# Attention with a gated feed-forward block on one core: pairs of token tiles by another seven-product scheme with two gathering PSUM banks, and a whole first gate

## The chip, the cores and the metric

The kernel runs on one NeuronCore of a Trainium2 chip. The core has five engines that run their own queues in order: TensorE (PE; its weight loads are shown apart as PEld), VectorE (DVE), ScalarE (ACT), GpSimd (POOL) and SyncE (SP, which here issues DMAs). The metric is the device time of one execution in microseconds; lower is better.

## The reference

Attention with a window of 96 positions and 8 global positions, then a feed-forward block with a ReLU gate on its output:

```python
B, H, S, D = 4, 8, 768, 64                 # q, k, v; n_global 8, n_local 96
keep = is_global | is_local
scores = scale * q @ k.T + bias            # bias: -slope of the head * distance
a = softmax(np.where(keep, scores, -1e9))
x = (a @ v) as [3072, 512]                 # tokens x (heads * 64)
gate = np.maximum(x @ w_gate, 0.0)         # w_gate, w_val: [512, 1536]
val = x @ w_val
out = (gate * val) @ w_out                 # w_out: [1536, 512], result fp32
```

## The kernel before

The 3072 tokens are cut into eight halves c = 0 to 7 (half a sequence each, 384 tokens, three tiles of 128). Per half there are two stages.

*Attention of a half* (`attention_pieces`): for each of four pairs of heads, scores on TensorE into `x_ps` banks (L397), Exp on ScalarE (L406), masks on VectorE (L359), the product with the values and its row sums on TensorE (L427), the reciprocal of the sums as Ln (L436) and Exp (L441) on ScalarE, and two multiplications on VectorE that normalise the result into the transposed activations `xT` (L446).

*Feed-forward of a half* (`ffn_pieces`): twelve chunks fc of 128 hidden columns. `gate(fc)` is four matmuls over `xT` into an `ff_ps` bank and a ReLU on ScalarE (L525). `val(fc)` is four matmuls and a multiplication on VectorE (L531) that writes `ht`, the hidden activations in bf16. Matmuls of both are at L518. Then comes the output product with w_out (`wo_sb`):

- the third token tile by 12 plain matmuls of 512 columns (`outp`, L538), copied out by ScalarE (L543); half 0 does all three tiles so
- the first two token tiles together by Strassen's scheme: the two tiles and the two halves of w_out's rows and columns make a 2x2 problem, done with 7 products of 6 matmuls of 256 columns (`block`, L583) in place of 8. VectorE makes sums of `ht` beforehand (`cb`, `ad`, `de`; L567, L571, L576), and, once, five sums of w_out (`bs`, L809). Products p4, p3, p1 are copied to the output tile `osb` by ScalarE (L599, L603, L607); p2 and p5 are added and subtracted there by VectorE (L611 to L617); p6 and p7 go on accumulating in the banks of p3 and p1 and are added last (L624, L629). They run in the order p4, p3, p1, p2, p5, p6, p7.

Halves 2 to 7 begin with `begin`: three quarters of gate 0 and of val 0 by turns, then the last quarter of each.

PSUM holds three `ff` and five `x` banks of 128x512 fp32. Buffers are handed out by turns, so an allocation waits until the one three (five) before it is read.

The order of all work is written by hand. `ffn_pieces(c)` gives a list of (weight, function); `weave` calls them in order and, when the summed weight passes a place, calls the attention pieces of the next half (`spread` gives their places, up to 0.8 of half c) and the loads and key transposes of the half after it (`early_pieces`, 0.25 to 0.75). Sums of `ht` stand behind certain `val` pieces (`behind`) or between output pieces (`f2.insert`). Each engine's queue is in this order: an instruction that waits holds all behind it. Output tiles are stored by SP's DMA queue; in half 7 one of four stores is on ScalarE's.

Of the kernel before, what the change touches and what calls it, by code (L numbers as in the profile page):

```python
# [8 lines left out]
FP32 = mybir.dt.float32  # L9
BF16 = mybir.dt.bfloat16  # L10
AF = mybir.ActivationFunctionType
ALU = mybir.AluOpType
# [3 lines left out]
def kernel(  # L16
# [12 lines left out]
    nc = tc.nc  # L29
# [14 lines left out]
    NHALF = 2 * B  # L44
# [27 lines left out]
    late = {}  # L72

    PSUM = bass.MemoryType.PSUM
    psum = {}
# [20 lines left out]
    wo_sb = const.tile([128, N_FC, DM], BF16)  # L96
# [409 lines left out]

    begin_of = {}

    def ffn_pieces(c):
        ht = ht_pool.tile([128, N_FC, QH], BF16, name="ht")  # L510
        st = {}
# [38 lines left out]
            if c == 2:  # L550
                product(wg, "g", 1, 0, N_DC - 1)


        N2, D2 = N_FC // 2, DM // 2
        tiles_ = [slice(n * 128, (n + 1) * 128) for n in range(2)]

        def sums_of(name, *shape):
            if name not in st:
                st[name] = late["sums"].tile([128, *shape], BF16, name=name)
            return st[name]  # L560

        cb = lambda: sums_of("cb", N2, 2, 128)
        ad = lambda: sums_of("ad", N2, 128)
        de = lambda: sums_of("de", N_FC, 128)

        def sum_cb(i0, i1):
            nc.vector.tensor_tensor(cb()[:, i0:i1].rearrange("f i n t -> f i (n t)"), ht[:, i0:i1, 0:256],  # L567
                                    ht[:, N2 + i0 : N2 + i1, 0:256], op=ALU.add)

        def sum_ad(i0, i1):  # L570
            nc.vector.tensor_tensor(ad()[:, i0:i1], ht[:, i0:i1, tiles_[0]],  # L571
                                    ht[:, N2 + i0 : N2 + i1, tiles_[1]], op=ALU.add)

        def sum_de(i0, i1):
            x, y = (1, 0) if i0 < N2 else (0, 1)
            nc.vector.tensor_tensor(de()[:, i0:i1], ht[:, i0:i1, tiles_[x]], ht[:, i0:i1, tiles_[y]],  # L576
                                    op=ALU.subtract)

        def block(key, pool, left, right, start, stop):
            if start:  # L580
                st[key] = psum[pool].tile([128, 512], FP32, name=f"{pool}_ps")
            for i in range(N2):
                nc.tensor.matmul(st[key][:, 0:D2], lhsT=left(i), rhs=right(i),  # L583
                                 start=start and i == 0, stop=stop and i == N2 - 1,
                                 skip_group_check=not start)
            return st[key][:, 0:D2]

        c0, c1 = slice(0, D2), slice(D2, DM)
        bs = lambda name: lambda i: late["bs"][name][:, i]
        V2 = nc.vector.tensor_tensor  # L590

        def store(n, cols, eng=nc.sync):
            eng.dma_start(out=out_v[c, n][:, cols], in_=st["r", n][:, cols])

        def p4():
            for n in range(2):
                st["r", n] = late["osb"].tile([128, DM], FP32, name="osb")
            ps = block("d", "ff", lambda i: ht[:, N2 + i, tiles_[1]], bs("b21-b11"), True, True)
            nc.scalar.copy(st["r", 0][:, c0], ps)  # L599

        def p3():
            ps = block("c", "ff", lambda i: ht[:, i, tiles_[0]], bs("b12-b22"), True, True)
            nc.scalar.copy(st["r", 0][:, c1], ps)  # L603

        def p1():
            ps = block("a", "ff", lambda i: ad()[:, i], bs("b11+b22"), True, True)
            nc.scalar.copy(st["r", 1][:, c1], ps)  # L607

        def p2():
            ps = block("b", "x", lambda i: cb()[:, i, 1], lambda i: wo_sb[:, i, c0], True, True)  # L610
            V2(st["r", 1][:, c0], ps, st["r", 0][:, c0], op=ALU.add)  # L611
            V2(st["r", 1][:, c1], st["r", 1][:, c1], ps, op=ALU.subtract)

        def p5():
            ps = block("e", "x", lambda i: cb()[:, i, 0], lambda i: wo_sb[:, N2 + i, c1], True, True)
            V2(st["r", 0][:, c1], ps, st["r", 0][:, c1], op=ALU.add)
            V2(st["r", 0][:, c0], st["r", 0][:, c0], ps, op=ALU.subtract)  # L617
            if c == NHALF - 1:
                store(1, c0)
                store(0, c1)  # L620

        def p6():
            ps = block("c", "ff", lambda i: de()[:, i], bs("b11+b12"), False, True)
            V2(st["r", 1][:, c1], ps, st["r", 1][:, c1], op=ALU.add)  # L624
            store(1, slice(0, DM) if c < NHALF - 1 else c1, nc.sync if c < NHALF - 1 else nc.scalar)

        def p7():
            ps = block("a", "ff", lambda i: de()[:, N2 + i], bs("b21+b22"), False, True)
            V2(st["r", 0][:, c0], ps, st["r", 0][:, c0], op=ALU.add)  # L629
            store(0, slice(0, DM) if c < NHALF - 1 else c0)  # L630

        behind = {2: [lambda: sum_de(0, 3)], 5: [lambda: sum_de(3, 6)], 8: [lambda: sum_cb(0, 3)],
                  9: [lambda: sum_ad(0, 3)], 10: [lambda: sum_de(6, 9)]}

        def val_and_sums(fc):
            val(fc)
# [8 lines left out]
        f2 = [(0.65, lambda n=n, part=part: outp(n, part))  # L645
              for n in (range(NN) if c < 1 else (NN - 1,)) for part in range(4)]
# [135 lines left out]
    for f in ("m1 g0 m3 v0 m2 g1 K3 K2 m0 g3 K1 S30 S31 g2 K0 S20 v3 S11 v1 S21 A3 N3 v2 S00 S01 "  # L782
# [10 lines left out]
        else:  # L793
# [8 lines left out]
    late["bs"] = {name: pool.tile([128, N_FC // 2, DM // 2], BF16, name=f"bs{i}")  # L802
                  for i, name in enumerate(("b21-b11", "b12-b22", "b11+b22", "b11+b12", "b21+b22"))}

    def wo_sum(name, part):
        i = slice(part * N_FC // 4, (part + 1) * N_FC // 4)
        x, y = (wo_sb[:, (int(b[1]) - 1) * N_FC // 2 :][:, i, (int(b[2]) - 1) * DM // 2 : int(b[2]) * DM // 2]
                for b in (name[:3], name[4:]))
        nc.vector.tensor_tensor(late["bs"][name][:, i], x, y, op=ALU.add if "+" in name else ALU.subtract)  # L809
# [9 lines left out]
    for f in (*casts[:7], lambda: nc.gpsimd.tensor_copy(held, wo_sb[0:1, N_FC - 1, 0:1]),  # L819
# [8 lines left out]
    weave(f1_0[G[2]] + f1_1[G[2]] + f2_0 + f2_1 + [(0.0, pieces.pop()[1])],  # L828
          [(0.33, order_k[2]), (0.38, order_k[3])],
          pieces, spread(early_pieces(3), 0.58, 0.88),  # L830
          spread([(0.0, lambda name=name, part=part: wo_sum(name, part)) for name in late["bs"] for part in range(2)],
                 0.1, 0.74))

    for c in range(2, NHALF):
        placed = []
        if c + 1 < NHALF:
            placed.append(spread(attention_pieces(c + 1), *((0.07, 0.82) if c == 2 else (0.0, 0.8))))
        if c + 2 < NHALF:
            load_qk(c + 2, 0, H)
            load_v_half(c + 2)  # L840
            placed.append(spread(early_pieces(c + 2), 0.25, 0.75))
        f1, f2 = ffn_pieces(c)
        weave(f1 + f2, *placed)

# [34 lines left out]
```

## Time and profile before

| | |
|---|---|
| median of 3 runs | 241.96 us (241.34 to 242.21) |
| the profiled execution | 241.74 us, of it 239.9 us from first to last instruction |
| granted TensorE clock | 0.998 of full speed |
| first matmul of the products of halves 1 to 7 | 71.8, 100.0, 126.9, 154.6, 181.6, 209.1, 231.9 us |
| first gate of halves 3 to 7 | 104.6, 131.5, 159.2, 186.2, 213.7 us |
| gate and val matmuls (L518) | 768, 53% of the chain that ended last |
| plain output product (L538) | 9% of that chain |
| Strassen products (L583) | 294 matmuls, 11% of that chain |
| VectorE: ht (L531), mean of one | 96, 554 ns |
| VectorE: output additions (L611 to L629) | 42, 409 to 425 ns |
| ScalarE: relu (L525), mean of one | 96, 492 ns |
| ScalarE: copies of products (L599, L603, L607) | 21, 370 to 374 ns |

In a line of the timeline the columns are the start in us from the span's beginning, the length in us, the engine, the line of the kernel, the operation, output<-input, and the shape; several like instructions that follow each other are one line with their count. In a line of stretches they are the stretch, its length, then for each engine its busy time and instructions (PE, PEld, DVE, ACT, POOL), the granted clock, the share of the DMA engines and GB/s. In the chain of waits they are start, length, engine, output, line and count. Matmuls are pipelined: one starts before the one ahead of it has ended.

### The profile page before, as it was taken

To read this page: it belongs to the slowest core of one execution; us is meant where nothing else is said; L and a number is where in the kernel's file an instruction comes from. 1 tells how busy PE (TensorE), PEld (TensorE's weight loads), DVE (VectorE), ACT (ScalarE), POOL (GpSimd) and SP (SyncE) were. 2 spreads that over 40 slices of the span, in tenths; PEclk is the share of its full clock that TensorE was granted. 3 is DMA by queue.
4 is the path that set the end of the run, shared out by engine and by line. 5 is a ranking of instruction groups with operands and counts; after the bars stand their busy time and mean duration, and the time that the engine had idled before them with its cause. 6 is when DMAs were issued, how large, how long until landed. Compare 5 with 4: busy or idle time off the path is not lost.

```text
span 239.9 us, 5355 instructions
## 1 busy us (share of the span) xinstructions
PE 233.5 (97%) x1937; PEld 146.6 (61%) x1945; DVE 173.3 (72%) x456; ACT 153.4 (64%) x347; POOL 85.9 (36%) x202
## 2 busy tenths in 40 slices
PE   7899999999999999999999999999999999999994
PEld 3655555665458566666668566676658566676663
DVE  7775955869677788777787687866887677764643
ACT  5897883337775777748774777638774677733330
POOL 6767893208414860903274060902350000000000
PEclk9999999999999999999999999999999999999999
DMA  6999999993976997098519939398431200030003
GB/s 200 181 198 177 257 234 219 185 162 61 270 178 134 301 150 131 8 185 257 108 25 122 285 93 133 19 166 262 67 68 44 90 0 0 3 129 3 4 27 104
DMA packets 69603, 31.42 MB, mean 131 GB/s; under 512 B 47160, under 2 KB 66616, under 8 KB 69576
## 3 DMA queue, kind: packets, MB, share of 16 engines
q0 software_dynamic: 31744, 8.71, 35.3%
q1 hardware_dynamic: 36616, 21.45, 35.1%
q10 hardware_dynamic: 1216, 0.92, 1.2%
q8 instruction: 15, 0.25, 0.4%
q14 instruction: 12, 0.10, 0.1%
HBM read 28.41 MB, written 6.29 MB: 145 GB/s over the span
## 4 chain that ended last, share of the span: by engine, by line
PE 91%; ACT 3%; DVE 2%; issue 1%; ACTq 0%
PE ff_ps L518 53%; PE ff_ps L538 9%; PE ff_ps L583 8%; PE x_ps L427 6%; PE x_ps L397 4%; PE x_ps L583 3%; PE t_ps L459 2%; PE s_ps L341 2%; PE t_ps L272 1%; PE t_ps L682 1%; ACT lnd L436 1%; PE t_ps L310 1%; DVE xT L446 1%; PE s_ps L321 1%; ACT rcp L441 0%
## 5 line engine op out<-in xcount | busy, mean ns | idle before, releaser
L518 PE MATMUL ff_ps<-xT,wg 128*128 128x384 bf16 x384 | 80.7, 326 | 0.5 <-ACT grelu L525 0.4
L518 PE MATMUL ff_ps<-xT,wv 128*128 128x384 bf16 x384 | 80.2, 326 | 0.0
L531 DVE TENSOR_TENSOR ht<-ff_ps,grelu 128x384 bf16<-128x384 f32 x96 | 53.1, 554 | 28.5 <-PE ff_ps L518 13.8
L525 ACT ACTIVATE grelu<-ff_ps 128x384 bf16<-128x384 f32 x96 | 47.1, 492 | 39.4 <-PE ff_ps L518 20.9
L518 PEld LDWEIGHTS <-wg 128*128 128x128 bf16 x384 | 35.9, 98 | 23.9 <-issue 0.9
L518 PEld LDWEIGHTS <-wv 128*128 128x128 bf16 x384 | 36.1, 97 | 23.4 <-issue 1.2
L406 ACT ACTIVATE es<-x_ps 128x360 bf16<-128x360 f32 (+2 forms) x96 | 36.8, 444 | 16.9 <-PE x_ps L397 16.8
L359 DVE TENSOR_TENSOR es<-es,m_all 128x432 bf16<-128x432 bf16 (+4 forms) x108 | 31.2, 334 | 8.2 <-ACT es L406 7.8
L446 DVE TENSOR_TENSOR xT<-x_ps,rcp 64x384 bf16<-64x384 f32 x48 | 26.6, 554 | 9.4 <-ACT rcp L441 8.8
L436 ACT ACTIVATE lnd<-x_ps 64x384 f32<-64x384 f32 x48 | 23.3, 485 | 12.5 <-PE x_ps L427 11.8
L538 PE MATMUL ff_ps<-wo_sb,ht 128*128 128x512 bf16 x112 | 29.6, 379 | 0.4
L363 POOL CAST kqc<-ks 128x384 bf16<-128x384 f32 x24 | 11.6, 532 | 32.3 <-DMA ks<-in_k_dram 32.3
L137 POOL DMA_DIRECT2D vbuf<-in_v_dram x25 | 21.6, 880 | 2.6 <-DMA wv<-in_moe_w_val_dram 2.1
L427 PE MATMUL x_ps<-es,vbuf 128*128 128x216 bf16 (+4 forms) x216 | 21.8, 225 | 0.0
L427 PEld LDWEIGHTS <-vbuf 128*128 128x128 bf16 x216 | 15.8, 97 | 7.7
L538 PEld LDWEIGHTS <-ht 128*128 128x128 bf16 x120 | 10.8, 97 | 9.8 <-issue 0.2
L263 POOL COPY kT<-kqT 128x240 bf16<-128x240 bf16 x16 | 6.9, 430 | 23.0 <-DMA kqT<-kqc 20.5
L363 POOL CAST kqc<-qs 128x384 bf16<-128x384 f32 x24 | 11.6, 522 | 8.1 <-DMA qs<-in_q_dram 8.1
L259 POOL COPY kT<-kqT 128x360 bf16<-128x360 bf16 x10 | 6.0, 604 | 19.9 <-DMA kqT<-kqc 19.9
L441 ACT ACTIVATE rcp<-lnd 128x384 f32<-128x384 f32 x24 | 12.6, 524 | 0.7
L347 ACT ACTIVATE ef<-s_ps 128x720 bf16<-128x720 f32 (+2 forms) x16 | 10.9, 710 | 2.1 <-PE s_ps L341 1.8
L397 PE MATMUL x_ps<-kqT,kT 64*128 64x216 bf16 (+4 forms) x216 | 11.8, 224 | 0.2
(115 smaller groups left out, 252.8 us busy)
## 6 DMA issues: line engine op xcount, KB each, us to landing
out_dram<-osb SPq DMA_DIRECT2D x22, 256.0 KB, 2.7
ks<-in_k_dram SPq DMA_DIRECT2D x6, 768.0 KB, 5.5
qs<-in_q_dram SPq DMA_DIRECT2D x6, 768.0 KB, 12.1
vbuf<-in_v_dram POOLq DMA_DIRECT2D x21, 120.0 KB, 7.9
wg<-in_moe_w_gate_dram POOLq DMA_DIRECT2D x3, 512.0 KB, 7.9
wv<-in_moe_w_val_dram POOLq DMA_DIRECT2D x3, 512.0 KB, 9.8
wo_sb<-in_moe_w_out_dram POOLq DMA_DIRECT2D x1, 1536.0 KB, 19.6
kq<-in_q_dram ACTq DMA_DIRECT2D x2, 192.0 KB, 4.7
```

The source lines that it names most:

```text
L137: nc.gpsimd.dma_start(out=v_dst(b, NG + r0, NG + r0 + n, j), in_=v[b, :, KT * j + r0 : KT * j + r0 + n, :].rearrange("h p d -> p h d"))
L359: nc.vector.tensor_mul(for_all, for_all, mk)
L363: nc.gpsimd.tensor_copy(kqc[:, :, i].rearrange("t n (h d) -> t h n d", d=D)[:, 2 * p : 2 * p + 2], of[s][:, 2 * p : 2 * p + 2, :].rearrang ...
L406: nc.scalar.activation(es[:, e, 0:c], banks[e][:, 0:c], AF.Exp, bias=0.0, scale=scale)
L427: nc.tensor.matmul(av3[:, :, a : a + w], lhsT=vb[:, j, z0 : z0 + 128], rhs=es[:, e, c : c + NN * w].rearrange("k (n p) -> k n p", n=NN), s ...
L436: nc.scalar.activation(ln[o0 : o0 + 64], av[d0 : d0 + 64, 0:QH], AF.Ln, bias=0.0, scale=1.0)
L446: nc.vector.tensor_tensor(xT_of[s][r, p, :], av_of[s, p, e][r, 0:QH], av_of[s, p, "r"][r], op=ALU.mult)
L518: nc.tensor.matmul(st[key][:, 0:QH], lhsT=w_of(w, dc, fc), rhs=xT_of[c][:, dc, :], start=(dc == 0), stop=(dc == N_DC - 1))
L525: nc.scalar.activation(gr, psg[:, 0:QH], AF.Relu, bias=0.0, scale=1.0)
L531: nc.vector.tensor_tensor(ht[:, fc, :], psv[:, 0:QH], st["gr", fc], op=ALU.mult)
L538: nc.tensor.matmul(ps2, lhsT=ht[:, fc, n * 128 : (n + 1) * 128], rhs=wo_sb[:, fc, :], start=(fc == 0), stop=(fc == N_FC - 1))
L583: nc.tensor.matmul(st[key][:, 0:D2], lhsT=left(i), rhs=right(i), start=start and i == 0, stop=stop and i == N2 - 1, skip_group_check=not s ...
```

## The change

The seven products follow another scheme (`winograd`): four sums s1 to s4 of `ht` and four sums t1 to t4 of w_out, each partly built on the one before, and four additions to the output. Three products (m1, m2 and m4) use a token tile as it is, three (m1, m2, m3) a part of w_out as it is. Products 6 and 7 accumulate onto product 1 in its bank, product 3 onto product 5 in its bank (`block` with `start` False); ScalarE copies out the states in between (m1, m5, m6, and m4), VectorE does the additions. Banks "a" and "b" are `ff` banks, "c" and "d" are `x` banks. The order is 1, 5, 6, 4, 2, 7, 3, and 1, 5, 6, 4, 7, 2, 3 in half 7. Sums stand at other places. Halves 3 to 7 begin with an ordinary gate 0 and val 0; half 2 keeps `begin`. The output pool has four buffers for three. A path for pairing third tiles is there, switched off by `PAIRED = ()`.

```diff
+    def winograd(pair, sums, order):
...
+        def add(j, i0=0, i1=N2):
+            lower, upper = slice(i0, i1), (N2 + i0, N2 + i1)
+            x, y, op = {1: lambda: (h(1, i0, i1), h(1, *upper), ALU.add),
+                        2: lambda: (s(1)[:, lower], h(0, i0, i1), ALU.subtract),
+                        3: lambda: (h(0, i0, i1), h(1, i0, i1), ALU.subtract),
+                        4: lambda: (h(0, *upper), s(2)[:, lower], ALU.subtract)}[j]()
+            V2(s(j)[:, lower], x, y, op=op)
...
+        def block(key, left, right, start=True):
+            if start:
+                pool = "ff" if key in "ab" else "x"
+                st[key] = psum[pool].tile([128, 512], FP32, name=f"{pool}_ps")
+            for i in range(N2):
+                nc.tensor.matmul(st[key][:, 0:D2], lhsT=left(i), rhs=right(i),
+                                 start=start and i == 0, stop=i == N2 - 1, skip_group_check=not start)
+            return st[key][:, 0:D2]
...
+        def m1():
+            nc.scalar.copy(r(0, 0), block("a", raw(0, 0), of_b(0, c0)))
+
+        def m2():
+            V2(r(0, 0), block("c", raw(0, 1), of_b(1, c0)), r(0, 0), op=ALU.add)
+            if last:
+                store(0, c0, nc.scalar)
+
+        def m3():
+            V2(r(0, 1), block("b", of_s(4), of_b(1, c1), False), r(0, 1), op=ALU.add)
+            store(0, c1 if last else slice(0, DM))
+
+        def m4():
+            nc.scalar.copy(r(1, 0), block("d", raw(1, 1), of_t(4)))
+
+        def m5():
+            nc.scalar.copy(r(1, 1), block("b", of_s(1), of_t(1)))
+
+        def m6():
+            nc.scalar.copy(r(0, 1), block("a", of_s(2), of_t(2), False))
+
+        def m7():
+            ps = block("a", of_s(3), of_t(3), False)
+            V2(r(1, 0), ps, r(1, 0), op=ALU.subtract)
+            V2(r(1, 1), ps, r(1, 1), op=ALU.add)
+            store(1)
+
+        return add, [(0.65, (m1, m2, m3, m4, m5, m6, m7)[i - 1]) for i in order]
+
+    PAIRED = ()
...
-        def p4():
-            for n in range(2):
-                st["r", n] = late["osb"].tile([128, DM], FP32, name="osb")
-            ps = block("d", "ff", lambda i: ht[:, N2 + i, tiles_[1]], bs("b21-b11"), True, True)
-            nc.scalar.copy(st["r", 0][:, c0], ps)
...
-        def p6():
-            ps = block("c", "ff", lambda i: de()[:, i], bs("b11+b12"), False, True)
-            V2(st["r", 1][:, c1], ps, st["r", 1][:, c1], op=ALU.add)
-            store(1, slice(0, DM) if c < NHALF - 1 else c1, nc.sync if c < NHALF - 1 else nc.scalar)
...
-        behind = {2: [lambda: sum_de(0, 3)], 5: [lambda: sum_de(3, 6)], 8: [lambda: sum_cb(0, 3)],
-                  9: [lambda: sum_ad(0, 3)], 10: [lambda: sum_de(6, 9)]}
+        plain = range(NN) if c < 1 else () if c - c % 2 in PAIRED else (NN - 1,)
+        add, products = winograd([(c, ht, 0), (c, ht, 1)], "sums", (1, 5, 6, 4, 7, 2, 3) if c == NHALF - 1 else
+                                 (1, 2, 5, 6, 4, 7, 3) if c in PAIRED else (1, 5, 6, 4, 2, 7, 3))
+        behind = {5: [lambda: add(3)], 8: [lambda: add(1, 0, 3)], 9: [lambda: add(2, 0, 3)],
+                  10: [lambda: add(4, 0, 3)]}
+        rest = tuple(lambda j=j: add(j, 3, 6) for j in (1, 2, 4))
...
-        if c >= 2:
-            f1[:2] = [(1.0, begin_of[c][0]), (0.15, begin_of[c][1]), (0.15, begin_of[c][2])]
         if c == 2:
-            f1[0] = (1.5, f1[0][1])
+            f1[:2] = [(1.5, begin_of[c][0]), (0.15, begin_of[c][1]), (0.15, begin_of[c][2])]
             f1[3] = (0.15, lambda: gate(1, N_DC - 1))
         if c >= 1:
-            f2 += [(0.65, f) for f in (p4, p3, p1, p2, p5, p6, p7)]
-            for at, f in ((5, lambda: sum_de(9, 12)), (3, lambda: sum_cb(3, 6)), (2, lambda: sum_ad(3, 6))):
+            f2 += (products3 if c - 1 in PAIRED else []) + products
+            places = (2, 3, 5) if plain else (0, 1, 2) if c in PAIRED else (0, 1, 2, 3)
+            for at, f in list(zip(places, rest))[::-1]:
                 f2.insert(at, (0.0, f))
...
-    late["osb"] = ctx.enter_context(tc.tile_pool(name="osb", bufs=3, reuse_waits="tile"))
+    late["osb"] = ctx.enter_context(tc.tile_pool(name="osb", bufs=4, reuse_waits="tile"))
...
+    late["sums3"] = ctx.enter_context(tc.tile_pool(name="sums3", bufs=1, reuse_waits="tile"))
+    late["t"] = {j: pool.tile([128, N_FC // 2, DM // 2], BF16, name=f"t{j}") for j in range(1, 5)}
+
+    def wo_sum(j, part):
+        n2 = N_FC // 2
+        i = slice(part * n2 // 2, (part + 1) * n2 // 2)
+        b = lambda upper, cols: wo_sb[:, upper * n2 : (upper + 1) * n2][:, i, cols]
+        t = {k: late["t"][k][:, i] for k in late["t"]}
+        x, y, op = {1: (b(0, c1), b(0, c0), ALU.subtract), 2: (t[3], b(0, c0), ALU.add),
+                    3: (b(1, c1), b(0, c1), ALU.subtract), 4: (t[2], b(1, c0), ALU.subtract)}[j]
+        nc.vector.tensor_tensor(t[j], x, y, op=op)
...
-          spread([(0.0, lambda name=name, part=part: wo_sum(name, part)) for name in late["bs"] for part in range(2)],
+          spread([(0.0, lambda j=j, part=part: wo_sum(j, part)) for j in (1, 3, 2, 4) for part in range(2)],
                  0.1, 0.74))
```

More of the change, by code (lines that the diff above doesn't have):

```diff
@@ L507, with h, s, r @@
     begin_of = {}
+    c0, c1 = slice(0, DM // 2), slice(DM // 2, DM)
+    V2 = nc.vector.tensor_tensor
+    def winograd(pair, sums, order):
+        N2, D2 = N_FC // 2, DM // 2
+        st = {}
+        last = pair[0][0] == NHALF - 1 and pair[0][2] == 0
+        def h(i, f0, f1):
+            _, ht, n = pair[i]
+            return ht[:, f0:f1, n * 128 : (n + 1) * 128]
+        def s(j):
+            if j not in st:
+                st[j] = late[sums].tile([128, N2, 128], BF16, name=f"s{j}")
+            return st[j]
+        def add(j, i0=0, i1=N2):
[5 more added lines that the diff above has]
+            V2(s(j)[:, lower], x, y, op=op)
+        def r(i, j):
+            if ("r", i) not in st:
+                st["r", i] = late["osb"].tile([128, DM], FP32, name="osb")
+            return st["r", i][:, (c0, c1)[j]]
+        def block(key, left, right, start=True):
[6 more added lines that the diff above has]
+            return st[key][:, 0:D2]
+        raw = lambda j, upper: lambda i: h(j, upper * N2 + i, upper * N2 + i + 1)[:, 0]
+        of_s = lambda j: lambda i: s(j)[:, i]
+        of_t = lambda j: lambda i: late["t"][j][:, i]
+        of_b = lambda upper, cols: lambda i: wo_sb[:, upper * N2 + i, cols]
+        def store(i, cols=slice(0, DM), eng=nc.sync):
+            c, _, n = pair[i]
+            eng.dma_start(out=out_v[c, n][:, cols], in_=st["r", i][:, cols])
+        def m1():
[19 more added lines that the diff above has]
+        return add, [(0.65, (m1, m2, m3, m4, m5, m6, m7)[i - 1]) for i in order]
@@ L509, in ffn_pieces @@
+    PAIRED = ()
+    third_of = {}
     def ffn_pieces(c):
@@ L551, in begin @@
                 product(wg, "g", 1, 0, N_DC - 1)
[L554 to L593, printed above, removed]
-        def p4():
-            for n in range(2):
-                st["r", n] = late["osb"].tile([128, DM], FP32, name="osb")
-            ps = block("d", "ff", lambda i: ht[:, N2 + i, tiles_[1]], bs("b21-b11"), True, True)
-            nc.scalar.copy(st["r", 0][:, c0], ps)
@@ L601, in p3 @@
[L601 to L620, printed above, removed]
-        def p6():
-            ps = block("c", "ff", lambda i: de()[:, i], bs("b11+b12"), False, True)
-            V2(st["r", 1][:, c1], ps, st["r", 1][:, c1], op=ALU.add)
-            store(1, slice(0, DM) if c < NHALF - 1 else c1, nc.sync if c < NHALF - 1 else nc.scalar)
@@ L627, in p7 @@
[L627 to L630, printed above, removed]
-        behind = {2: [lambda: sum_de(0, 3)], 5: [lambda: sum_de(3, 6)], 8: [lambda: sum_cb(0, 3)],
-                  9: [lambda: sum_ad(0, 3)], 10: [lambda: sum_de(6, 9)]}
+        plain = range(NN) if c < 1 else () if c - c % 2 in PAIRED else (NN - 1,)
+        add, products = winograd([(c, ht, 0), (c, ht, 1)], "sums", (1, 5, 6, 4, 7, 2, 3) if c == NHALF - 1 else
+                                 (1, 2, 5, 6, 4, 7, 3) if c in PAIRED else (1, 5, 6, 4, 2, 7, 3))
@@ new lines, in ffn_pieces @@
+        behind = {5: [lambda: add(3)], 8: [lambda: add(1, 0, 3)], 9: [lambda: add(2, 0, 3)],
+                  10: [lambda: add(4, 0, 3)]}
+        rest = tuple(lambda j=j: add(j, 3, 6) for j in (1, 2, 4))
+        if c in PAIRED:
+            third_of[c] = ht
+        elif c - 1 in PAIRED:
+            add3, products3 = winograd([(c, ht, NN - 1), (c - 1, third_of[c - 1], NN - 1)], "sums3",
+                                       (1, 5, 6, 4, 2, 7, 3))
+            behind.update({1: [lambda: add3(1)], 6: [lambda: add3(2)], 7: [lambda: add3(3)]})
+            rest = (lambda: add3(4),) + rest
@@ L645, in ffn_pieces @@
         f2 = [(0.65, lambda n=n, part=part: outp(n, part))
-              for n in (range(NN) if c < 1 else (NN - 1,)) for part in range(4)]
-        if c >= 2:
-            f1[:2] = [(1.0, begin_of[c][0]), (0.15, begin_of[c][1]), (0.15, begin_of[c][2])]
+              for n in plain for part in range(4)]
         if c == 2:
-            f1[0] = (1.5, f1[0][1])
+            f1[:2] = [(1.5, begin_of[c][0]), (0.15, begin_of[c][1]), (0.15, begin_of[c][2])]
             f1[3] = (0.15, lambda: gate(1, N_DC - 1))
         if c >= 1:
-            f2 += [(0.65, f) for f in (p4, p3, p1, p2, p5, p6, p7)]
-            for at, f in ((5, lambda: sum_de(9, 12)), (3, lambda: sum_cb(3, 6)), (2, lambda: sum_ad(3, 6))):
+            f2 += (products3 if c - 1 in PAIRED else []) + products
+            places = (2, 3, 5) if plain else (0, 1, 2) if c in PAIRED else (0, 1, 2, 3)
+            for at, f in list(zip(places, rest))[::-1]:
                 f2.insert(at, (0.0, f))
@@ L799 @@
     pool = ctx.enter_context(tc.tile_pool(name="late", bufs=1, reuse_waits="tile"))
-    late["osb"] = ctx.enter_context(tc.tile_pool(name="osb", bufs=3, reuse_waits="tile"))
+    late["osb"] = ctx.enter_context(tc.tile_pool(name="osb", bufs=4, reuse_waits="tile"))
     late["sums"] = ctx.enter_context(tc.tile_pool(name="sums", bufs=1, reuse_waits="tile"))
[L802 to L809, printed above, removed]
+    late["sums3"] = ctx.enter_context(tc.tile_pool(name="sums3", bufs=1, reuse_waits="tile"))
[8 more added lines that the diff above has]
+        nc.vector.tensor_tensor(t[j], x, y, op=op)
     G = [slice(2 * GW * i, 2 * GW * (i + 1)) for i in range(N_FC // GW)]
@@ L830 @@
           pieces, spread(early_pieces(3), 0.58, 0.88),
-          spread([(0.0, lambda name=name, part=part: wo_sum(name, part)) for name in late["bs"] for part in range(2)],
+          spread([(0.0, lambda j=j, part=part: wo_sum(j, part)) for j in (1, 3, 2, 4) for part in range(2)],
                  0.1, 0.74))
+    ahead = {}
     for c in range(2, NHALF):
         placed = []
-        if c + 1 < NHALF:
-            placed.append(spread(attention_pieces(c + 1), *((0.07, 0.82) if c == 2 else (0.0, 0.8))))
         if c + 2 < NHALF:
@@ L841 @@
             placed.append(spread(early_pieces(c + 2), 0.25, 0.75))
+        if c + 1 < NHALF:
+            pieces = ahead.pop(c + 1, None) or attention_pieces(c + 1)
+            if c in PAIRED:
+                placed.append([(0.76, pieces[-2][1]), (0.84, pieces[-1][1])])
+                placed.append(spread(pieces[:-2], 0.07, 0.735))
+            else:
+                placed.append(spread(pieces, *(0.07, 0.82) if c == 2 else (0.0, 0.8)))
+        if c + 1 in PAIRED:
+            ahead[c + 2] = attention_pieces(c + 2)
+            placed.append(spread([ahead[c + 2].pop(0) for _ in range(3)], 0.82, 0.93))
         f1, f2 = ffn_pieces(c)
```

## The prediction

> **What bounds the kernel now.** I read the page first (busy shares and slices), then the chain that ended last in order of time, then stretches by half with the granted clock, and last the timeline around the products of each half. Halves are counted by c, 0 to 7.
>
> ```profile
> PE 233.5 (97%) x1937; PEld 146.6 (61%) x1945; DVE 173.3 (72%) x456; ACT 153.4 (64%) x347; POOL 85.9 (36%) x202
> PE 91%; ACT 3%; DVE 2%; issue 1%; ACTq 0%
> ...
> 127.11 1.97 PE ff_ps L583 x18
> ...
> 213.85 15.60 PE ff_ps L518 x96
> ...
> 131.69:159.36 27.67, 27.56 (x232) 17.85 (x230) 21.47 (x54) 18.98 (x44) 9.93 (x23) 1.00 0.72 132
> ```
>
> TensorE is busy for 97% and makes up 91% of the chain. Inside the chain the matmuls stream: 15.60 us over 96 is 0.1625 us for 384 columns, 1.97 over 18 is 0.109 us for 256 columns. Half 4, the stretch from 131.69 to 159.36, is busy for 27.56 of 27.67 us at a granted clock of 1.00. So VectorE and ScalarE cost time only where a matmul starts later than its predecessor's pace allows. A stall under 0.3 us does not show as idle, because the modelled end of a matmul hides it; it is read from start times. From 57 us on, I find seven such stalls, 1.5 us together, each named below.
>
> **The change, part by part.** The number of matmuls does not move: 84+84+84+42 = 294 at L583 before, 7 halves of 7 products of 6 after. TensorE's own work is therefore equal, and only waits can change the time.
>
> *Sums and additions.* Per half VectorE drops from 4 sums of `de` (0.392), 2 of `cb` (0.554) and 2 of `ad` (0.355), 3.39 us, to one of 768 elements (0.554) and six of 384 (0.355 to 0.392), 2.7 to 2.9 us. Sums of wo fall from 10 to 8 at 0.553, so 1.1 us once. Output additions fall from 6 to 4 at 0.42, so 0.8 us a half, and ScalarE gets one copy more at 0.37. I price all of it at nothing: in the page VectorE idles 28.5 us ahead of L531, 13.8 of it for TensorE itself, and the cover is a matmul stream that does not wait for it. Two stalls do hang on VectorE's masks, 0.20 us at 152.66 and 0.12 at 179.80, where the mask is queued behind the last product of val, which came from TensorE just before; less work earlier does not move that. Bounds: 0 to -0.3 us.
>
> *Two banks.* This is the added wait. Product 6 accumulates into the bank of product 1, so it cannot begin before ScalarE has copied product 1 out; only product 5, six matmuls, lies between. Before, product 6 came back to the bank of product 3 with three products between. The built program's order of instructions puts the copy of product 1 exactly where the copy of p4 (L599) stood on ScalarE: behind the last Ln, Exp and the output copy L543. So the start of the third product before (12 matmuls after the first) against the end of L599 tells the wait:
>
> ```profile
> 100.03 1.47 PE L583 MATMUL ff_ps<-bs,ht 128*128 128x256 bf16 x12
> ...
> 101.05 0.52 ACT L441 ACTIVATE rcp<-lnd 128x384 f32<-128x384 f32 x1
> 101.34 0.82 PE L583 MATMUL ff_ps<-bs,ad 128*128 128x256 bf16 x6
> 101.47 0.35 ACT L599 COPY osb<-ff_ps 128x256 f32<-128x256 f32 x1
> ```
>
> ```profile
> 127.44 0.57 ACT L543 COPY osb<-ff_ps 128x512 f32<-128x512 f32 x1
> ...
> 127.90 0.38 ACT L599 COPY osb<-ff_ps 128x256 f32<-128x256 f32 x1
> 128.25 0.82 PE L583 MATMUL ff_ps<-bs,ad 128*128 128x256 bf16 x6
> ```
>
> Release costs 0.05 us: below, a relu ends at 133.63+0.50 = 134.13 and the matmul that waited for it starts at 134.18. In half 2 product 6 wants 101.34 and gets 101.47+0.35+0.05 = 101.87: +0.53. In half 3 it wants 128.25 and gets 127.90+0.38+0.05 = 128.33: +0.08. The same rows of halves 4, 5 and 6 (copies at 155.57, 182.59, 210.06; products at 155.92, 182.94, 210.41) also give 0.08, so +0.32 for four. Half 1 has eight attention matmuls between products 5 and 6, so the copy (73.16+0.37) is in time for 73.62; but its copy of product 6 falls behind two Ln and an Exp, where L607 stood, 75.28+0.35+0.05 = 75.68 against 75.58 for product 7: +0.10, and the next half's first gate, which waits for the last normalisation behind VectorE's additions, moves with it. In half 7 the copies are done 0.04 us before products 6 and 7 want their bank (233.15 against 233.19): 0. Behind a waiting product 6 stand the other products and the next half's gates on TensorE; ScalarE and VectorE then wait for those, so nothing takes up the delay. Together +0.95; bounds 0.6 (no wait in halves 3 to 6) to 1.3 (0.17 in each of them).
>
> *Whole gate.* In half 4 the split beginning delays both first groups, ScalarE takes two exps before the relu, and val 1 finds its bank still held:
>
> ```profile
> 133.34 0.81 PE L518 MATMUL ff_ps<-xT,wg 128*128 128x384 bf16 x4
> 133.63 0.50 ACT L525 ACTIVATE grelu<-ff_ps 128x384 bf16<-128x384 f32 x1
> ...
> 134.18 0.81 PE L518 MATMUL ff_ps<-xT,wv 128*128 128x384 bf16 x4
> ```
>
> Four matmuls from 133.34 end their stream at 133.99, the next begins at 134.18: 0.19 lost, and 0.18 likewise at 188.69 in half 6. Halves 3, 5 and 7 lose nothing there. With a whole gate the relu is queued ahead of the exps and the bank is free some 1 us before val 1 wants it: -0.37 for two halves. The scores that follow move 2 matmuls, 0.33 us, ahead; GpSimd's key copies for half 3 ended at 99.27, 5 us earlier, so they cover it. xT of a half is complete before its first gate in halves 3 to 7: the last normalisation of half 3 ends at 102.72, the half begins at 104.61. Bounds -0.37 to 0 (a new wait in place of the old one).
>
> *Tail.* Before, the last half leaves in four stores of 128 KB, issued at 235.21, 235.87, 236.53 (ScalarE's queue) and 237.11. After, 256 KB go at about 236.1, 128 KB at 236.5 on ScalarE's queue, and the last 128 KB at 237.1, since the last addition still follows the last product. The packets of the 256 KB store of 232.69 took 0.83 us, those of a 128 KB store 0.51; the first packet comes 0.85 us after the issue. The two earlier stores then have some 240 KB left at 237.4, about 0.8 us, so they overrun the last one's first packet (237.96) by 0.15 to 0.25 us. I take +0.15; bounds 0 to 0.4.
>
> A fourth output buffer and the unused second pool cost nothing: stores land in 1.7 to 5.9 us, and a buffer comes round after a half of 26 us or more. The paired third tiles are never built.
>
> **Sum.** 0.95 - 0.37 + 0.15 = +0.73 us. The profiled span 239.9 becomes 240.7; its execution took 241.74, so 242.47; the median of the runs, 241.96, lies 0.22 above that execution: 242.7 us.
>
> **The skill on waits like these.** The granted clock stayed at 1.00 over half 4 in spite of its 0.19 and 0.20 us stalls, so I add nothing for the clock. The Trainium skill, page "TensorE: Matmul & The Clock Gate", section "A second HAM failure mode: psum-queue depth-cycling", says that short idle spells between matmul groups that cycle through PSUM banks made the clock swing between half and full. By its window of about 3.4 us, an estimate from that page, each of six waits could cost up to 1.7 us, some 10 us in all, 252 us. No row here shows such a swing.
>
> **Rivals.** (B) The waits for the copies are not felt, because product 1's copy is dispatched earlier than p4's was: then 0 for the banks, -0.37 and +0.15: 241.7. For it: ScalarE has idle time there in half 7. Against: its queue is in order and the rows ahead of the copy do not change. (C) Slower: the copy is late in halves 3 to 6 too, as in half 2, because more than the Exp stands ahead of it; 5 x 0.53 + 0.10 - 0.37 + 0.15 = +2.5, 244.5. It decides from a mean wait of 0.2 us in those four halves ((1.21 - 0.53 - 0.10 + 0.37 - 0.15)/4). For it: a margin of only 0.03 us; against: four halves with equal rows. (D) Faster: the stalls before were VectorE's lateness after all; without the two of 0.20 and 0.12, two of 0.26 at the scores of half 2 (63.41, 68.67), 0.25 at 78.19, 0.37 at the gates, no wait for copies and the tail: -1.46+0.15 = -1.3, 240.7. Against: these end with ScalarE's Exp or TensorE's own val, not with a sum.
>
> **How the numbers follow.** Half a per cent, 1.2 us, is about what a measurement of this kernel tells from no change. Chances: forecast 0.62, B 0.18, C 0.14, D 0.06. Faster is D, 0.06. Slower is C and the upper end of the forecast, 0.14 + 0.04 = 0.18. No change 0.76. The forecast's own bounds are 0.6-0.37 = 0.2 to 1.3+0.4 = 1.7 us, 242.2 to 243.7; down to B with the spread of the runs, 241.5 to 243.7.
>
> **What would show it.** In the trace after: the first matmul of product 6 starts 0.05 us after the copy of product 1 ends in halves 2 to 6, 0.5 us late in half 2 and under 0.1 us in the others; no late val 1 in halves 4 and 6; equal granted clock; the last packets 0.15 us later. It is wrong if product 6 streams on without a gap, if the waits in halves 3 to 6 exceed 0.2 us, or if the scores at the start of a half wait.

## The result and the profile after

The changed kernel takes 242.5 us (median of 22 runs, 242.01 to 243.5) against 241.66 us for the kernel before, run beside it (22 runs, 240.86 to 242.95). The ratio is 1.0038, with a 95% interval of 1.0027 to 1.0049: slower by 0.92 us (0.65 to 1.18). That is clear of zero, and inside the half per cent (1.2 us) that the prediction counts as no change. The forecast was 242.7 us and +0.73. The profiled execution has a span of 240.5 us, 0.57 more than before, and a granted clock of 1.00.

The page after, busy time and the chain's shares by engine:

```profile
PE 233.6 (97%) x1945; PEld 146.3 (61%) x1945; DVE 163.3 (68%) x433; ACT 156.4 (65%) x354; POOL 87.4 (36%) x202
PE 88%; DVE 4%; DMA 3%; ACT 2%; issue 1%; ACTq 0%; DVEq 0%
```

VectorE gave up 10 us of busy time (173.3 before) and TensorE's did not move. The same over about one half, the stretch from 100.0 to 127.4 us, which begins with the products of half 2 and ends within those of half 3 (columns as in the stretches shown before), first of the kernel before:

```profile
100.00:127.40 27.40, 27.35 (x222) 17.89 (x220) 20.30 (x51) 19.13 (x46) 11.81 (x27) 1.00 0.63 128
```

and of the kernel after:

```profile
100.00:127.40 27.40, 27.02 (x217) 17.39 (x215) 19.02 (x48) 19.13 (x46) 11.60 (x26) 1.00 0.62 127
```

VectorE is 1.28 us lighter; TensorE gets five matmuls less done and idles 0.33 us more. What it waits for is in the view of waits (engine, what it wanted, whom it waited for: us in total, times, longest). The second of these lines is new:

```profile
PE ff_ps L602 <- ACT grelu L609: 0.4, 1, 0.4
PE ff_ps L547 <- ACT osb L561: 0.4, 1, 0.4
```

L561 is the copy of product 1, L547 the products. The timeline of half 2 shows that wait:

```profile
99.95 0.82 PE L547 MATMUL ff_ps<-wo_sb,ht 128*128 128x256 bf16 x6
...
100.97 0.52 ACT L441 ACTIVATE rcp<-lnd 128x384 f32<-128x384 f32 x1
101.40 0.35 ACT L561 COPY osb<-ff_ps 128x256 f32<-128x256 f32 x1
...
101.81 0.81 PE L547 MATMUL ff_ps<-t,s 128*128 128x256 bf16 x6 [0.38 <-ACT osb L561]
```

The copy stands behind an Exp (L441), ends at 101.75, and product 6 starts at 101.81. Its predecessor, product 5, started at 100.61 and would have let it go at 101.26. So 0.55 us are lost, of which the profile calls only 0.38 idle, since the modelled end of a matmul covers the rest.

I took all such losses from the start times: the step from one matmul to the next, less 0.160 us for 384 columns of the first and in proportion for others (long streams run at 0.1625). They are, in us:

| place | before | after | forecast |
|---|---|---|---|
| product 7 of half 1 | 0 | 0.11 | 0.10 |
| first val of half 2 | 0 | 0.09 | not priced |
| scores of half 2 at 88 us | 0.10 | 0.30 | 0 |
| product 6 of half 2 | 0 | 0.55 | 0.53 |
| product 6 of halves 3 to 6 | 0 | 0.08, 0.08, 0.09, 0.08 | 0.08 each |
| val 1 of halves 4 and 6 | 0.19, 0.19 | 0, 0 | 0, 0 |
| last matmul's start to the end | 3.59 | 3.81 | +0.15 |
| VectorE's masks (152.7, 179.8) or gate (145.2) | 0.20, 0.12 | 0.29 | as before |

The late val 1 is gone in half 4 of the kernel after: val 1 follows 0.65 us behind gate 1, the pace of four matmuls.

```profile
132.06 0.81 PE L602 MATMUL ff_ps<-xT,wg 128*128 128x384 bf16 x4
132.80 0.48 PE L397 MATMUL x_ps<-kqT,kT 64*128 64x216 bf16 x10
133.21 0.82 PE L602 MATMUL ff_ps<-xT,wv 128*128 128x384 bf16 x4
133.87 0.81 PE L602 MATMUL ff_ps<-xT,wg 128*128 128x384 bf16 x4
134.52 0.81 PE L602 MATMUL ff_ps<-xT,wv 128*128 128x384 bf16 x4
```

Without the last row of the table, whose stalls wander (below), that is +1.11. The row of the scores at 88 us wanders too (below), so its +0.20 is that of these two executions. The span shows only 0.57, above all because its first product started 0.44 us earlier (71.32 against 71.76): over the three executions of the old form that were profiled this start lies between 71.26 and 71.76, over the eleven of the new form between 71.28 and 72.74, so the 0.44 looks like chance.

### The profile page after: what moved, and what is told of

Its sections match the earlier page's. It is cut to its first block, busy times and chain, and to the rows that moved or that the text cites. A ratio compares the mean times of both kernels' runs of the same rounds, so it can differ in the third digit from the quotient of the medians.

```text
span 240.5 us, 5330 instructions
## 1 busy us (share of the span) xinstructions
PE 233.6 (97%) x1945; PEld 146.3 (61%) x1945; DVE 163.3 (68%) x433; ACT 156.4 (65%) x354; POOL 87.4 (36%) x202
## 4 chain that ended last, share of the span: by engine, by line
PE 88%; DVE 4%; DMA 3%; ACT 2%; issue 1%; ACTq 0%; DVEq 0%
PE ff_ps L602 51%; PE ff_ps L622 10%; PE ff_ps L547 9%; PE x_ps L427 5%; PE x_ps L397 4%; PE x_ps L547 4%; DMA kq<-in_q_dram 3%; PE t_ps L459 2%; PE t_ps L310 1%; PE s_ps L341 1%; DVE xT L446 1%; PE t_ps L272 1%; ACT lnd L436 1%; DVE ht L615 1%; DVE s L535 1%
## 5 line engine op out<-in xcount | busy, mean ns | idle before, releaser
L602 PE MATMUL ff_ps<-xT,wg 128*128 128x384 bf16 x384 | 79.0, 326 | 0.6 <-ACT grelu L609 0.4
L602 PE MATMUL ff_ps<-xT,wv 128*128 128x384 bf16 x384 | 78.6, 326 | 0.0
L406 ACT ACTIVATE es<-x_ps 128x360 bf16<-128x360 f32 (+2 forms) x96 | 36.2, 443 | 4.6 <-PE x_ps L397 4.6
L446 DVE TENSOR_TENSOR xT<-x_ps,rcp 64x384 bf16<-64x384 f32 x48 | 26.6, 554 | 10.3 <-ACT rcp L441 9.5
L359 DVE TENSOR_TENSOR es<-es,m_all 128x432 bf16<-128x432 bf16 (+4 forms) x108 | 30.5, 330 | 3.1 <-ACT es L406 2.9
L547 PEld LDWEIGHTS <-s 128*128 128x128 bf16 x168 | 16.3, 97 | 2.9 <-issue 0.6
L547 PE MATMUL ff_ps<-t,s 128*128 128x256 bf16 x126 | 16.7, 272 | 0.4 <-ACT osb L561 0.4
L622 PEld LDWEIGHTS <-ht 128*128 128x128 bf16 x120 | 10.9, 97 | 9.5
L363 POOL CAST kqc<-qs 128x384 bf16<-128x384 f32 x24 | 12.6, 565 | 9.9 <-DMA qs<-in_q_dram 9.9
L547 PEld LDWEIGHTS <-ht 128*128 128x128 bf16 x126 | 12.3, 98 | 2.7
L441 ACT ACTIVATE rcp<-lnd 128x384 f32<-128x384 f32 x24 | 12.6, 523 | 0.8
```

Of the source, the lines that this page charges most:

```text
L359: nc.vector.tensor_mul(for_all, for_all, mk)
L363: nc.gpsimd.tensor_copy(kqc[:, :, i].rearrange("t n (h d) -> t h n d", d=D)[:, 2 * p : 2 * p + 2], of[s][:, 2 * p : 2 * p + 2, :].rearrang ...
L406: nc.scalar.activation(es[:, e, 0:c], banks[e][:, 0:c], AF.Exp, bias=0.0, scale=scale)
L446: nc.vector.tensor_tensor(xT_of[s][r, p, :], av_of[s, p, e][r, 0:QH], av_of[s, p, "r"][r], op=ALU.mult)
L602: nc.tensor.matmul(st[key][:, 0:QH], lhsT=w_of(w, dc, fc), rhs=xT_of[c][:, dc, :], start=(dc == 0), stop=(dc == N_DC - 1))
L622: nc.tensor.matmul(ps2, lhsT=ht[:, fc, n * 128 : (n + 1) * 128], rhs=wo_sb[:, fc, :], start=(fc == 0), stop=(fc == N_FC - 1))
```

## The experiments

All ratios are against the kernel before, on the same chip; the first batch's median for it is 241.44 us, the second's 241.54, the third's 241.37, the last's 241.50.

| kernel | median, us | ratio (95% interval) |
|---|---|---|
| changed kernel, first time | 242.5 | 1.0038 (1.0027 to 1.0049) |
| changed kernel, again | 242.51 | 1.0040 (1.0024 to 1.0055) |
| far: 1,5,4,6,2,7,3 in halves 1 to 6 | 242.26 | 1.0033 (1.0020 to 1.0047) |
| near: 1,6,5,4,2,7,3 | 247.15 | 1.0234 (1.0211 to 1.0256) |
| far but in half 1 | 241.74 | 1.0015 (1.0000 to 1.0030) |
| split gate kept | 243.31 | 1.0082 (1.0061 to 1.0104) |
| before, with the whole gate | 241.26 | 0.9993 (0.9977 to 1.0009) |
| the same, again | 241.0 | 0.9980 (0.9967 to 0.9994) |
| s3 in two pieces | 242.91 | 1.0052 (1.0038 to 1.0065) |
| far but in half 1, s3 in two | 241.57 | 1.0002 (0.9989 to 1.0016) |
| the same, tail stored in two | 241.35 | 1.0007 (0.9988 to 1.0026) |
| one store less (one run) | 242.16 | |
| no casts of late queries (one run) | 242.49 | |

**The copy waits: farther and nearer.** Product 4 between 5 and 6 gives the copy of product 1 six matmuls more; product 6 straight after 1 gives it none.

```
- (1, 2, 5, 6, 4, 7, 3) if c in PAIRED else (1, 5, 6, 4, 2, 7, 3)
+ (1, 2, 5, 6, 4, 7, 3) if c in PAIRED else (1, 5, 4, 6, 2, 7, 3)    far
+ (1, 2, 5, 6, 4, 7, 3) if c in PAIRED else (1, 6, 5, 4, 2, 7, 3)    near
```

Far: 

> The changed kernel with product 4 moved between products 5 and 6 in halves 1 to 6 (order 1, 5, 4, 6, 2, 7, 3), nothing else. Theory (product 6 waits for ScalarE's copy of product 1): the waits of 0.55 us in half 2, 0.08 in each of halves 3 to 6 and 0.11 in half 1 go, together 0.99; so 1.0 us less than the changed kernel, 241.5, within 0.2 us of before. Rival (the new sums on VectorE and the stores at the end make the kernel slower, and a wait at product 6 is taken up by later slack): no change against the changed kernel, 242.5.

Near: 

> The changed kernel with product 6 right behind product 1 in halves 1 to 6 (order 1, 6, 5, 4, 2, 7, 3), so that nothing lies between product 1 and the wait for its copy. Theory: the wait grows by the 0.655 us of product 5 in halves 2 to 6 and from 0.11 to about 1.1 in half 1, some 4.2 us, 246.7 us, and the granted clock stays at 1.00. Rival (later slack takes waits up): under 1 us more. If short idle spells made the clock swing, more than 8 us more and a granted clock under 0.95.

Near cost 4.7 us (1.0234 less 1.0038), and its view of waits names it:

```profile
PE ff_ps L547 <- ACT osb L561: 4.3, 6, 1.0
```

From the first product to the end its profiled execution is 4.3 us longer than the changed kernel's, at a clock of 0.999. By the start times of the matmuls its six waits are 0.74 to 1.20 us, 5.3 us together, 4.3 more than in the changed kernel; the profile's longest, 1.0, leaves out what the modelled ends cover. So waits for that copy go into the time in full, and six of up to 1.2 us bring no swing of the clock. Far missed its forecast: 0.1 us in the timed runs where 1.0 was expected, as its rival had it. Its trace tells part of the reason. Product 6 waits nowhere in halves 2 to 6, as expected, but in half 1 the wait went on to product 7 and grew from 0.11 to 0.39 us:

```profile
74.51 0.52 ACT L441 ACTIVATE rcp<-lnd 128x384 f32<-128x384 f32 x1
74.58 0.82 PE L547 MATMUL x_ps<-wo_sb,ht 128*128 128x256 bf16 x6
74.94 0.35 ACT L573 COPY osb<-x_ps 128x256 f32<-128x256 f32 x1
...
75.20 0.38 ACT L579 COPY osb<-ff_ps 128x256 f32<-128x256 f32 x1
...
75.62 0.81 PE L547 MATMUL ff_ps<-t,s 128*128 128x256 bf16 x6 [0.23 <-ACT osb L579]
```

Both copies stand behind Ln and Exp there, and the far order puts the copy that nobody waits for (L573, product 4) ahead of the one that product 7 needs (L579, product 6). From its first product to the end, far's profiled execution is 0.69 us shorter than the changed kernel's (168.50 against 169.19). The timed runs show less of that than the trace; their intervals overlap widely, and why they show less stays open.

**Far, but not in half 1.**

```
+ (1, 5, 6, 4, 2, 7, 3) if c == 1 else (1, 5, 4, 6, 2, 7, 3)
```

> Order 1,5,4,6,2,7,3 in halves 2 to 6, and the changed kernel's own 1,5,6,4,2,7,3 in half 1, where the far order moved the wait to product 7 (0.39 us there against 0.11, because ScalarE's copies of products 4 and 6 stood behind two normalisations). Theory (the copy waits are the cost of the change): 0.88 us less matmul idleness than the changed kernel, so about 241.6. Rival (the waits only take up slack that another engine would take anyway, as the far order's small gain in the timed runs, 0.2 us, suggests): 242.2 or more.

Measured beside the changed kernel itself, run again as a yardstick:

> The changed kernel itself, unaltered, as the yardstick for the three that follow on the same chip. Expected 0.92 us over the kernel before, as measured first. In its trace product 6 of half 2 waits some 0.55 us, products 6 of halves 3 to 6 some 0.08 each, product 7 of half 1 some 0.11. What may differ from the first profile are the stalls that come from VectorE's bf16 work beside GpSimd (0.29 at the gate of half 4 at 145 us there): if they are chance of one execution, they are elsewhere or gone here.

The yardstick's copy waits were 0.546, 0.079, 0.080, 0.079, 0.080 and 0.109 us: the same as in the first profile to 7 ns. It is 1.0040, this one 1.0015: 0.6 us less by the ratios, 0.77 by the medians, against 0.88 expected. Half 2 in the far order, where product 6 is the fourth line of TensorE:

```profile
101.56 0.82 PE L547 MATMUL ff_ps<-wo_sb,ht 128*128 128x256 bf16 x6
102.21 0.82 PE L547 MATMUL ff_ps<-t,s 128*128 128x256 bf16 x6
102.87 0.82 PE L547 MATMUL x_ps<-t,ht 128*128 128x256 bf16 x6
...
103.00 0.35 ACT L561 COPY osb<-ff_ps 128x256 f32<-128x256 f32 x1
...
103.52 0.82 PE L547 MATMUL ff_ps<-t,s 128*128 128x256 bf16 x6
```

The copy ends at 103.35, product 6 starts at its own pace at 103.52. The theory holds: about two thirds of the 0.97 us, or four fifths by the medians, were the late copy. The two intervals touch (1.0024 to 1.0055 and 1.0000 to 1.0030), so the share is rough.

**The whole gate, taken back and put in alone.** One kernel keeps the split beginning in the new form; one has the whole gate in the kernel before and nothing else of the change.

```
+        if c >= 2:
+            f1[:2] = [(1.0, begin_of[c][0]), (0.15, begin_of[c][1]), (0.15, begin_of[c][2])]
         if c == 2:
-            f1[:2] = [(1.5, begin_of[c][0]), (0.15, begin_of[c][1]), (0.15, begin_of[c][2])]
+            f1[0] = (1.5, f1[0][1])
```

Split kept: 

> The changed kernel with the split beginning kept in halves 3 to 7. Theory: the late val 1 of halves 4 and 6 comes back, 0.19 us each, so 0.4 us more than the changed kernel, 242.9. Rival (the whole gate gains nothing, the late val 1 came from where the waits fell before): no change, 242.5.

Whole gate alone: 

> The kernel before with whole gates in halves 3 to 7 and its own scheme of products. Theory: the two waits of 0.19 us go, 0.4 us less than before, 241.3. Rival: the gain is bound to the new scheme, which leaves the banks in another turn; here val 0 and gate 1 take banks that products 6 and 7 have just left, and it is no faster or slower than before.

Whole gate alone, again: 

> The kernel before with the whole gate at the start of halves 4, 6 and the others, alone, on another chip than the first time (241.26 against 241.44). Theory: the two stalls of 0.19 us at the first val of halves 4 and 6 go, 0.37 us less than the kernel before. Rival: no change, since VectorE's wandering stalls take it back.

Alone, the whole gate gave 0.17 us the first time, within the error, and 0.48 us the second (0.14 to 0.80), around the 0.37 forecast; the two late val 1 are gone from both traces. The split beginning in the new form cost 1.06 us, more than the 0.4 expected. Half 4 of that kernel:

```profile
133.57 0.49 PE L602 MATMUL ff_ps<-xT,wg 128*128 128x384 bf16 x2
133.98 0.48 PE L602 MATMUL ff_ps<-xT,wv 128*128 128x384 bf16 x2
...
135.47 0.81 PE L602 MATMUL ff_ps<-xT,wg 128*128 128x384 bf16 x4
136.30 0.81 PE L602 MATMUL ff_ps<-xT,wv 128*128 128x384 bf16 x4
```

Two matmuls of 384 columns stream in 0.33 us, but the first val starts 0.41 us after the first gate: its bank is the one of product 7, which VectorE still reads for its two additions (L583, L584; the second ends at 133.92). That is 0.09 us in each of five halves. Four matmuls stream in 0.65, but val 1 comes 0.83 after gate 1, the old 0.19, and the same in half 6. Together 0.81 us. So in the new form the whole gate is worth 0.8 us, not 0.37: a split beginning wants val's bank 0.33 us after its first gate begins, a whole one after four matmuls and, in halves 3 to 7, the scores (in half 4 of the changed kernel the gate starts at 132.06 and val at 133.21), when VectorE is through. Half 2, which keeps the split, pays the 0.09 in the changed kernel too. The 0.25 us left over is within the error of the timed runs.

**The sum s3 in two pieces.**

```
- behind = {5: [lambda: add(3)],
+ behind = {2: [lambda: add(3, 0, 3)], 5: [lambda: add(3, 3, 6)],
```

> The sum s3 in two pieces of 384 columns, behind val 2 and val 5, in place of one of 768 columns behind val 5; nothing else. Theory (the one-piece sum delays VectorE's normalisation and so the scores of half 2, and VectorE's masks of half 4): the 0.30 us stall of the scores near 87.9 us falls back to 0.10, and the gate's 0.29 near 145 us goes; 0.2 to 0.5 us less than the changed kernel, 242.0 to 242.3. Rival (those stalls come from GpSimd's casts alone and move about): no change, 242.5.

No gain: 1.0052 against 1.0040. The scores of half 2 waited 0.39 us, between the two profiles of the changed kernel (0.30 and 0.41). They wait for the normalisation (L446), which VectorE does straight after the sum, so I put the duration of the sum beside that wait for all the executions:

| execution | the sum there, us | wait of the scores, us |
|---|---|---|
| before | 0.36 (`de`, 384) | 0.10 |
| before with the whole gate, twice | 0.70, 0.71 | 0.44, 0.46 |
| after, twice | 0.56, 0.67 (s3, 768) | 0.30, 0.41 |
| far, near, split gate kept, one store less, no casts of late queries | 0.56 each | 0.30 each |
| far but in half 1 | 0.85 | 0.60 |
| s3 in two pieces, alone | 0.65 (384) | 0.39 |
| s3 in two, in the two last kernels | 0.36 | 0.10 |

The wait is the duration less 0.26 us, every time. An undisturbed s3 in one piece costs 0.2 us more than an undisturbed half sum: that part comes with the change. The rest comes and goes, in the old form as well. On average the two forms hardly differ: three profiles of the old one wait 0.33 us, seven of the new one with s3 in one piece and all casts wait 0.36. What the longer piece costs in the median of the timed runs is therefore not shown.

**What stretches VectorE's sums.** In the far order but for half 1 the sum took 0.85 us:

```profile
87.06 1.86 POOL L363 CAST kqc<-qs 128x384 bf16<-128x384 f32 x4 [0.83 <-DMA qs<-in_q_dram]
...
88.47 0.85 DVE L535 TENSOR_TENSOR s<-ht 128x768 bf16<-128x768 bf16 x1
```

GpSimd casts the queries at that time, from 87.06 to 88.92, once their load is in, and that moment differs between executions. Leaving those casts out for halves 4 to 7 tests it (these halves compute with stale queries):

```
     def piece_cast(s, p, i):
+        if i == 1 and s >= 4:
+            return
```

> The changed kernel with GpSimd's casts of the queries left out for halves 4 to 7, so that those halves compute with stale queries. Theory (VectorE's bf16 work out of SBUF is stretched where such a cast lies beside it): the sum s3 of half 2, near 87.5 us, takes 0.56 us, in place of the 0.56, 0.67 and 0.85 of three runs, the scores after it wait 0.30 or less where they waited up to 0.60, and the overlapped masks come nearer to their free durations. Rival (the stretch comes from somewhere else, DMA traffic for one): sums and masks still vary up to 0.7 us at the same places.

```profile
84.31 1.63 POOL L365 CAST kqc<-ks 128x384 bf16<-128x384 f32 x3
```

```profile
87.66 0.56 DVE L537 TENSOR_TENSOR s<-ht 128x768 bf16<-128x768 bf16 x1
```

The first is all that GpSimd does from 84.5 to 91 us in this kernel, the second its s3: 0.56 us, and the scores wait 0.30, as the theory says. By itself that proves little, since five of the seven profiles with the casts and s3 in one piece have 0.56 as well.

What the fourteen profiles do show is that the order decides. The sum was stretched in five of them, and in these a cast had begun before it and had 0.26 to 0.51 us left to run; in the other nine no cast had more than 0.13 left when the sum began. Where a cast began during the sum, the sum kept its time, and the cast took 0.63 to 0.89 us in place of 0.51. In the kernel before the sum was first, by 0.08 us:

```profile
87.44 0.36 DVE L576 TENSOR_TENSOR de<-ht 128x384 bf16<-128x384 bf16 x1
```

```profile
87.52 2.00 POOL L363 CAST kqc<-qs 128x384 bf16<-128x384 f32 x4 [1.72 <-DMA qs<-in_q_dram]
```

From 71 us on, the masks of 432 columns that lie beside GpSimd's work (seven, ten and nine of them) average 0.395 us in the kernel without the late query casts, against 0.486 and 0.471 in the two executions of the changed kernel, and 0.377 where GpSimd is quiet. Masks beside the key casts, which stayed, still reach 0.63. One execution each, so the size is rough.

**The tail.** The store of the last half's second block is left out (those 256 KB are not written):

```
             V2(r(1, 1), ps, r(1, 1), op=ALU.add)
-            store(1)
+            if not last:
+                store(1)
```

> The changed kernel with the store of the last half's second block left out (its 256 KB are not written). Read from the start of the last matmul to the end of the span: 3.59 us in the kernel before, 3.80 to 3.82 in every run of the new form. Theory (that block's store is bunched with the last two and its packets hold them up): 3.5 to 3.6. Rival (the last store is slower by itself): 3.8 as before the edit.

Issues of DMAs from 229 us on (KB each, median us from issue to landing), first the kernel after, then this one:

```profile
out_dram<-osb SPq DMA_DIRECT2D x2, 256.0 KB
out_dram<-osb ACTq DMA_DIRECT2D x1, 128.0 KB, 2.1
out_dram<-osb SPq DMA_DIRECT2D x1, 128.0 KB, 1.9
```

```profile
out_dram<-osb SPq DMA_DIRECT2D x1, 128.0 KB, 1.7
```

The last store lands in 1.7 us, where it took 1.9 behind the other two. In the kernel before it was 1.7 as well:

```profile
out_dram<-osb SPq DMA_DIRECT2D x3, 128.0 KB, 1.7
```

With the one store left out, the closing wait for the last store on SP starts 2.50 us after the last matmul's start, again as before (2.50), against 2.66 after. So 0.16 us of the tail is the bunched packets. The end came at 3.71, not at the 3.5 to 3.6 expected. In all three traces SP closes the program with nine such waits in turn, and the one for the last store is the sixth before, the fifth after and the fourth here. So three, four and five of them still follow it, at some 0.06 us each, even where they have nothing left to wait for: 0.06 us more after than before, and 0.12 here.

**Together.** Far but for half 1 and s3 in two pieces, once with the last half's second block stored in two pieces, once without:

```
+            if last:
+                store(1, c0)
             V2(r(1, 1), ps, r(1, 1), op=ALU.add)
-            store(1)
+            store(1, c1 if last else slice(0, DM))
```

With: 

> The far order in halves 2 to 6, s3 in two pieces, and the last half's second block stored in two pieces, the first as soon as its addition is done. Theory: the gains add (0.88 + 0.2 to 0.5 + 0.1): 241.0 to 241.4, below the kernel before. Rival (VectorE or the stores give it back): 241.7 or more.

Without: 

> The far order in halves 2 to 6 and s3 in two pieces, with the changed kernel's stores: the new form without its late copies. What stays against the kernel before with the whole gate alone (0.998 of the kernel before) is the tail (0.22), product 7 of half 1 (0.11) and val 0 of half 2 (0.09), 0.42 us. Theory (waits are all there is; VectorE's fewer sums are worth nothing): 1.000 of the kernel before, 241.4. Rival (VectorE's lighter load pays by itself): 0.998 or less, 241.0 or less.

1.0007 and 1.0002: both are level with the kernel before. The first was forecast below it, and is not shown to be; the second is where the theory put it (1.000). The tail in two pieces bought nothing that shows: its last store's closing wait does start at 2.49, but VectorE's closing step came some 0.2 us late in that execution (the profile of the second kernel has the same, with 4.02 us from the last matmul's start to the end), and its interval is wide. The best kernel of all is the one before with the whole gate, 0.9980 (0.9967 to 0.9994; 0.9993 the first time).

## Why the prediction was right, step by step

- **Two banks, +0.95.** Measured 0.55 + 0.33 + 0.11 = 0.99 us, each at its place; moving product 6 away in halves 2 to 6 took 0.88 of it out of the trace and 0.6 to 0.8 out of the timed runs. The row of the copy before (L599) told where the copy after (L561) would end, to 0.02 us.
- **"the next half's first gate ... moves with it".** Beyond that, the first val of half 2 waits 0.09 us for VectorE's two additions on product 7's bank. I had named the additions only for the normalisation behind them, not for the bank that they hold.
- **Whole gate, -0.37.** Confirmed in the traces, where both stalls went. In the timed runs the whole gate alone measures -0.17 (-0.56 to +0.22) and -0.48 (-0.80 to -0.14). Put in on top of the new form it is worth 0.8, which the sum did not need.
- **"I price all of it at nothing", bounds 0 to -0.3.** VectorE is indeed lighter by 10 us, and nothing came of it. But the range allows only a gain, and one step was left out: where a piece of 384 columns of `de` stood, s3 stands as one piece of 768, straight ahead of a normalisation that TensorE waits for. That is +0.20 us where nothing disturbs the two, and 0.03 on the average of the profiles, which is too little to tell from nothing. I had counted VectorE's total and not the longest piece in front of a due instruction.
- **Tail, +0.15.** 0.16 for the packets, as worked out, and 0.06 for one more closing wait behind the last store's: together 0.21.
- **Rival B** (waits not felt) and **C** (late by 0.5 in five halves) fell: the near order felt its longer waits in full, far but in half 1 got most of them back, and in halves 3 to 6 they were 0.08. **D** (VectorE's lateness was the old cost) fell too: the stalls at 63.4, 68.7 and 78.2 us stayed (0.26, 0.26, 0.23). Of the signs named for being wrong none came: product 6 waited, by no more than 0.09 us in halves 3 to 6, and the first scores of halves 3 to 6 do not wait (those at 88 us stand in the middle of half 2).
- **The swing of the clock** did not occur: the granted clock was 1.00 after, and 0.999 with six waits of up to 1.2 us. The swing that the Trainium skill tells of for another kernel (page "TensorE: Matmul & The Clock Gate", section "A second HAM failure mode: psum-queue depth-cycling") did not come with waits this short and few.

The forecast's sum was 0.73, the measured +0.92 (0.65 to 1.18). The three that it missed (0.09, 0.20, 0.06) make 0.35, the copy waits another 0.04, and with them the sum is the table's 1.11, to 0.01. With 0.03 for the scores in place of 0.20 it would be about 0.95; the timed runs cannot tell the two apart. That the time itself, 242.7 against 242.5, came so near is in part luck: the three runs of the kernel before that were known then have a median 0.30 us above that of the 22, which makes up for the 0.19 by which the difference was too small.

## What to carry to other kernels

Before a bank is reused after fewer products, find in the old trace the instruction that will release it, read its end, add the release time, and compare with the pace: this gave six waits to 0.02 us. When an order is changed to make room for one late reader, look at each half by itself, since a copy moved ahead of a more urgent one hands the wait on. When work on a lighter engine is gathered into fewer pieces, price the longest piece ahead of what the bounding engine waits for as well as the sum.

## What the runs showed of the hardware

VectorE's additions and masks with both inputs in SBUF (bf16) are stretched by GpSimd's casts and copies that began before them. In four traces (before, after, far but for half 1, no late query casts), from 71 us on, none of the 442 that had no such GpSimd work beside them took over 10% more than the shortest of its shape; of the 115 that had, 77 did, a 384-column sum up to 0.73 us for 0.36. Of these 115, 55 began while a cast or copy had over 0.2 us left to run, and all 55 were stretched; 13 began ahead of every cast or copy beside them, and none was. GpSimd then paid: of its 198 casts and copies with no such VectorE work beside them none took over 10% more than the median of its shape, of the 96 that began while one ran 72 did. Those that read PSUM did not move: the longest multiplication into ht took 0.559 us before and after, with GpSimd beside it and without. The Trainium skill, page "SBUF — State Buffer", section "Who interferes with whom", says that a VectorE instruction with two SBUF inputs contends with a GpSimd instruction that reads SBUF, and one with at most one (outside the modes that use both ports) does not: the traces agree. This is why stalls of 0.1 to 0.6 us wander between executions of one kernel here, and a reason to compare two profiles stall by stall before a difference in span is believed.
